# A new TensorE order table, new plan keys and another split of R tiles between VectorE and ScalarE in an attention plus two-FFN kernel

## The chip, the cores and the metric
The kernel runs on one core of a Trainium2 chip. The metric is device time in microseconds (us). Engines are named as in the profile: PE (TensorE matmul), PEld (its weight load), DVE (VectorE), ACT (ScalarE), POOL (GpSimd), SP (SyncE, which issues the DMAs).

## What is computed
Attention with a learned position bias, then two gated feed-forward networks, all in fp32 (2 batches, 8 heads, 576 positions, head width 64):

```python
x    = log1p(|i - j|) / log1p(max(i, 1))             # 576 x 576
bias = relu(x[..., None] @ w1 + b1) @ w2             # 32 hidden units -> 8 heads
e    = exp(s - max(s)), s = q @ k.T / 8 + bias
a    = (e / sum(e)) @ v                              # -> 1152 x 512
y    = (h * clip(h + 3, 0, 6) / 6) @ w_out,          h = a @ w_in
z    = rmsnorm(y) * g;  out = (silu(z @ w_gate) * (z @ w_val)) @ w_out2
```

## The kernel before
**Attention** is cut into 9 query tiles of 128 rows and, in each, 4 pairs of heads: 36 units, u = 0 to 35. A unit u is these blocks, which are also the names in the order table:
- S.u (`scores`, L440): four matmuls that multiply q by k for two heads; the two heads lie in the two row halves of the array. It writes two PSUM tiles `s`.
- softmax_d (L453, DVE, two per unit): adds the bias, writes e and the row extreme m. ACT then does exp (L464, two per unit).
- T.u.0, T.u.1, T.u.2 (`e_turn`, L101): 4, 4 and 1 transposes of e into PSUM (`tps`); e_copy (L484, DVE or ACT) evacuates each to `et`.
- PV.u (`pv`, L502): ten matmuls of v by `et`, accumulated in `pv`.

After the fourth unit of a tile come rps.t (transposes of the reciprocal sums) and on other engines rt, xf, xh (L540) and xl, which give the split input of the feed-forward networks. kT and qT are transposes of k and q; their evacuations are `kS` (L329) and `q` (L338).

**The bias** is made in 36 groups n of 16 positions. Each group needs four R tiles (`bias_R`: L357 on DVE, L352 on ACT, 128 rows by 304 to 576 columns), one block B.n of matmuls (L370), an evacuation `ev` in two parts (L393 on ACT, short parts L391 on DVE), a store to DRAM (L399) and, when eight groups are stored, loads back as `bias` (L425). Groups 16 to 23 come first; unit 0 waits for them.

**Order.** Every step has a key (PARAMS) and is emitted in order of key. Up to the key `man` that fixes the order on all engines. Behind it PE follows the table ORDER word for word, while a scheduler places the steps of the other engines, which work through their queues strictly in order. `START` and `MID` say by which engine (D is DVE, A is ACT) the four R tiles of a group are made; `ET` the same for e_copy by part and u mod 4, `KE` for the k evacuations, `XH` for xh. PSUM: two buffers for `s`, three for all transposes and the narrow B blocks, one for `pv`. SBUF: three `e`, three `et`, two `rawq`.

**The feed-forward networks** follow in a fixed order (L722, L767). Their weights are split into a high and a low part by ACT, DVE and POOL, a few of them already during attention.

Of the kernel before, what the change touches and what calls it, by code (L numbers as in the profile page):

```python
# [18 lines left out]
def shape_tables():  # L19
# [7 lines left out]


PARAMS = dict(
    g0=-5.972, gs=0.589, g8=-0.524, gt=-0.138, g14=1.055, gr=1.163, man=-0.96, zra=-0.643, zrd=-0.393, zrp=-1.107,  # L30
    zb=0.442, zev=0.711, zst=0.263, zevd=-77.57, zkt=-0.534, zkc=0.263, zqh=0.09, rd=-0.054, ra=-0.173, rp=0.346,
    b=0.242, ev=0.359, st=0.097, evd=82.888, k0=-5.351, k1=-3.46, k2=-2.983, k3=-0.198, k4=-0.333, k5=1.346,
    k6=2.548, k7=1.028, k8=2.644, lk=-2.593, cc=-5.654, kt=0.51, kc=0.179, lv0=0.532, lv1=1.209, q0=-3.292,
    q1=-0.365, q2=0.79, q3=4.828, lq1=-0.018, lq=-2.569, qa=0.311, qb=4.328, qh=0.06, bl=-5.532, s0=-0.452, s1=0.01,
    d0=0.245, d1=0.116, e0=0.934, e1=1.216, t0=0.919, t1=1.874, t2=1.529, c0=0.653, c1=0.389, c2=0.434, pv=2.825,
    ri=1.245, rb=1.468, rps=2.385, rt=2.634, xf=3.608, xh=4.242, xl=4.531, w=0.894, ws=0.496,
)

ORDER = """
kT.0,0,0 B.16 B.17 B.18 kT.0,1,0 B.19 kT.0,2,0 qT.0 B.21 B.22 B.23 B.20 S.0 B.13 B.12 B.11 B.10 B.9 kT.0,1,1  # L40
B.8 kT.0,0,1 qT.1 S.1 T.0.0 B.14 T.0.2 S.2 kT.1,0,0 T.1.0 T.0.1 kT.1,0,1 B.15 T.1.2 S.3 T.1.1 T.2.0 kT.1,1,0 B.24
kT.1,1,1 T.2.2 S.4 T.2.1 PV.0 PV.1 B.25 T.3.0 T.3.2 S.5 PV.2 qT.2 B.26 T.3.1 T.4.0 rps.0 T.4.2 S.6 B.27 B.28
PV.3 T.4.1 T.5.0 T.5.2 S.7 PV.4 T.5.1 T.6.0 T.6.2 S.8 PV.5 B.29 B.30 qT.3 T.7.0 T.7.2 T.6.1 S.9 PV.6 T.7.1
T.8.0 rps.1 T.8.2 S.10 T.8.1 B.32 B.31 PV.7 T.9.0 B.33 PV.8 T.9.1 T.9.2 S.11 T.10.0 T.10.2 S.12 T.11.0 qT.4
B.34 PV.9 T.10.1 T.11.2 S.13 PV.10 B.35 T.11.1 T.12.0 B.0 rps.2 T.12.2 T.13.0 S.14 PV.11 T.12.1 T.13.2 S.15 T.14.0
T.14.2 B.2 B.1 PV.12 T.14.1 T.13.1 S.16 PV.13 B.3 T.15.0 qT.5 T.15.2 S.17 B.4 PV.14 T.15.1 T.16.0 rps.3
T.16.2 S.18 B.5 PV.15 T.16.1 T.17.0 T.17.2 S.19 PV.16 T.17.1 T.18.0 B.7 T.18.2 B.6 S.20 PV.17 T.19.0 qT.6 
T.18.1 T.19.2 S.21 PV.18 T.19.1 T.20.0 rps.4 T.20.2 S.22 PV.19 T.20.1 T.21.0 T.21.2 S.23 PV.20 T.21.1 T.22.0 T.22.2
S.24 PV.21 T.22.1 T.23.0 qT.7 T.23.2 S.25 PV.22 T.23.1 T.24.0 rps.5 T.24.2 S.26 PV.23 T.24.1 T.25.0 T.25.2
S.27 PV.24 T.25.1 T.26.0 T.26.2 S.28 PV.25 T.26.1 T.27.0 qT.8 T.27.2 S.29 PV.26 T.27.1 T.28.0 rps.6 T.28.2  # L50
S.30 PV.27 T.28.1 T.29.0 T.29.2 S.31 PV.28 T.29.1 T.30.1 T.31.0 T.30.0 T.30.2 S.32 PV.29 T.31.2 S.33 PV.30
T.31.1 rps.7 T.32.0 T.32.2 S.34 PV.31 T.32.1 T.33.0 T.33.2 S.35 PV.32 T.33.1 T.34.0 T.34.2 PV.33 T.34.1 T.35.0 T.35.2
PV.34 T.35.1 rps.8 PV.35
"""

START = ["DDDD", "DDAA", "DDAD", "DDDA", "DDDD", "DDDA", "DDDA", "DDDD"]
MID = ["DDDD", "DDDA"]
ET = ["DADA", "DAAA", "DAAD"]
KE = ["D", "D"]
RB, RT, XH, XL = "PADP"  # L60
SLOTS = dict(wr=3, na=0, nb=8, ns=29, far=8)
BUFS = dict(rawk=3, rawq=2, qp=2, bp=5, ep=3, etp=3, sm=3, Rp=12, evp=4, xa=1, ps_s=2, ps_t=3, ps_v=1)

# [2 lines left out]
def kernel(ctx, tc, q, k, v, w1, b1, w2, w_in, w_out, w_gate, w_val, w_out2, rms_g, dtab, ntab, itab, out):  # L66
# [170 lines left out]
    if True:  # L237
# [333 lines left out]
        def at(key, name, needs, fn, *args):  # L571
            plan.append((key, len(plan), name, needs, fn, args))
# [10 lines left out]
        for i, n in enumerate(n for c in order for n in range(8 * c, min(8 * c + 8, NG))):  # L583
            g = group_key(i)
            z = "z" if i < 8 else ""
            R_eng[n] = "".join(sorted(START[i] if i < 8 else MID[i % len(MID)], key="PDA".index))
            for j, x in enumerate(sorted(range(4), key=lambda x: "PAD".index(R_eng[n][x]))):
# [14 lines left out]
        for i, (x, key) in enumerate(KK.items()):  # L602
# [329 lines left out]
```

## Time and profile before

| | us |
|---|---|
| median of 3 runs | 650.74 (650.61 to 651.8) |
| profiled execution | 649.78 |
| its span | 648.0 |
| first matmul of the feed-forward networks | 211.94 |

PE is busy for most of the span. A busy time says that an instruction was under way, not that the engine ran at its best rate; where a block of always the same matmuls takes longer than elsewhere, it waited inside. The start of unit u is found on PE's timeline as the u-th row group `s<-kS,q`: unit 5 starts at 53.25, unit 6 at 61.17, unit 22 at 149.76 us.

### The profile page before, as it was taken

To read this page: it belongs to the slowest core of one execution; us is meant where nothing else is said; L and a number is where in the kernel's file an instruction comes from. 1 tells how busy PE (TensorE), PEld (TensorE's weight loads), DVE (VectorE), ACT (ScalarE), POOL (GpSimd) and SP (SyncE) were. 2 spreads that over 40 slices of the span, in tenths; PEclk is the share of its full clock that TensorE was granted. 3 is DMA by queue.
4 is the path that set the end of the run, shared out by engine and by line. 5 is a ranking of instruction groups with operands and counts; after the bars stand their busy time and mean duration, and the time that the engine had idled before them with its cause. 6 is when DMAs were issued, how large, how long until landed. Compare 5 with 4: busy or idle time off the path is not lost.

```text
span 648.0 us, 10847 instructions
## 1 busy us (share of the span) xinstructions
PE 616.8 (95%) x4136; PEld 518.6 (80%) x4136; DVE 460.6 (71%) x852; ACT 335.6 (52%) x691; POOL 143.3 (22%) x114
## 2 busy tenths in 40 slices
PE   4688889998999999999999999999999999999997
PEld 2245556666777999999999999999899999999996
DVE  6975897757564899888843799969766761387812
ACT  4766757777665565555534555564444441253511
POOL 1000100113110243333310023423332330032400
PEclk9989999999999999999999999999999999999999
DMA  6998965537200244434320134443433340154301
GB/s 151 271 258 245 293 206 156 144 102 184 94 1 2 66 141 147 121 121 124 127 66 1 33 99 130 130 130 98 133 128 119 108 148 16 33 177 150 98 1 49
DMA packets 73952, 77.78 MB, mean 120 GB/s; under 512 B 31916, under 2 KB 58668, under 8 KB 73900
## 3 DMA queue, kind: packets, MB, share of 16 engines
q1 hardware_dynamic: 73636, 77.02, 40.2%
q8 instruction: 32, 0.52, 0.3%
q14 instruction: 20, 0.16, 0.1%
q10 hardware_dynamic: 264, 0.07, 0.0%
HBM read 63.83 MB, written 13.25 MB: 119 GB/s over the span
## 4 chain that ended last, share of the span: by engine, by line
PE 80%; ACT 5%; DVE 4%; DMA 4%; SPq 3%; issue 2%; POOL 0%; ACTq 0%; POOLq 0%; DVEq 0%
PE h L722 39%; PE ya L767 18%; PE yb L767 9%; PE s L440 5%; PE pv L502 3%; PE tps L101 3%; ACT e L464 3%; PE bps L370 2%; DVE e L453 2%; SPq L305 1%; DVE R L357 1%; ACT ev L393 1%; DMA rawq<-in_q_dram 1%; DMA raw<-in_moe_w_out_dram 1%; ACT et L484 1%
## 5 line engine op out<-in xcount | busy, mean ns | idle before, releaser
L166 POOL TENSOR_TENSOR wl<-wm,wh 128x512 fp32r<-128x512 f32 x85 | 125.5, 1477 | 298.8 <-ACT wh L137 184.2
L158 DVE SCALAR_TENSOR_TENSOR wm<-raw,wm 128x512 int32<-128x512 int32 x85 | 120.6, 1419 | 0.9
L731 ACT CAST gh<-r 128x384 fp32r<-128x384 f32 x84 | 43.2, 514 | 115.7 <-DVE r L754 68.8
L722 PE MATMUL h<-nh,wh 128*128 128x384 f32 x288 | 97.2, 338 | 0.0
L722 PE MATMUL h<-nh,wl 128*128 128x384 f32 x288 | 96.7, 336 | 0.0
L722 PE MATMUL h<-nl,wh 128*128 128x384 f32 x288 | 96.5, 335 | 0.0
L464 ACT ACTIVATE e<-e,m 128x576 f32<-128x576 f32 x72 | 55.4, 770 | 48.6 <-DVE m L453 48.6
L722 PE MATMUL h<-xh,wh 128*128 128x384 f32 x192 | 65.4, 340 | 0.0
L754 DVE TENSOR_TENSOR r<-r,h 128x384 f32<-128x384 f32 x36 | 19.9, 553 | 63.1 <-PE h L722 63.1
L722 PE MATMUL h<-xh,wl 128*128 128x384 f32 x192 | 64.7, 337 | 0.0
L722 PE MATMUL h<-xl,wh 128*128 128x384 f32 x192 | 64.5, 336 | 0.0
L453 DVE CUSTOM_DVE_ANT_0 e<-s,bias 128x576 f32<-128x576 f32 x72 | 51.7, 754 | 16.6 <-PE s L440 14.8
L154 DVE SCALAR_TENSOR_TENSOR wm<-raw,wm 128x512 int32<-128x512 int32 x85 | 60.9, 716 | 2.8
L734 DVE TENSOR_TENSOR gl<-r,gh 128x384 fp32r<-128x384 f32 x84 | 46.6, 555 | 16.8 <-ACT gh L731 16.8
L145 ACT ACTIVATE wm<-raw 128x512 f32<-128x512 f32 x85 | 57.2, 674 | 2.2 <-DMA raw<-in_moe_w_in_dram 1.3
L101 PE MATMUL tps<-ident,e 128*128 128x128 f32 x324 | 49.3, 284 | 7.1 <-ACT et L484 4.1
L722 PEld LDWEIGHTS h<-nh,wh 128*128 128x128 f32 x288 | 54.1, 188 | 2.3 <-DVE nl L831 0.9
L357 DVE TENSOR_SCALAR R<-T,NB 128x320 f32<-128x320 f32 (+17 forms) x124 | 49.9, 460 | 8.3 <-PE bps L370 8.2
L722 PEld LDWEIGHTS h<-nl,wh 128*128 128x128 f32 x288 | 54.1, 188 | 1.4
L722 PEld LDWEIGHTS h<-nh,wl 128*128 128x128 f32 x288 | 54.0, 188 | 0.0
L101 PEld LDWEIGHTS tps<-ident,e 128*128 128x128 f32 x324 | 35.6, 142 | 22.6 <-ACT et L484 7.5
L137 ACT CAST wh<-wm 128x512 fp32r<-128x512 f32 x85 | 52.3, 618 | 1.0 <-DVE wm L158 0.9
(95 smaller groups left out, 1051.3 us busy)
## 6 DMA issues: line engine op xcount, KB each, us to landing
raw<-in_moe_w_out_dram SPq DMA_DIRECT2D x33, 512.0 KB, 3.6
biasd<-ev SPq DMA_DIRECT2D x36, 295.5 KB, 4.2
raw<-in_moe_w_in_dram SPq DMA_DIRECT2D x18, 512.0 KB, 3.6
raw<-in_moe_w_gate_dram SPq DMA_DIRECT2D x18, 512.0 KB, 3.5
bias<-biasd SPq DMA_DIRECT2D x15, 576.0 KB, 4.5
raw<-in_moe_w_val_dram SPq DMA_DIRECT2D x16, 512.0 KB, 3.6
bias<-biasd SPq DMA_DIRECT2D x10, 288.0 KB, 3.9
rawk<-in_k_dram SPq DMA_DIRECT2D x18, 128.0 KB, 3.8
```

The source lines that it names most:

```text
L101: nc.tensor.transpose(out, in_, ident[:n, :n])
L137: nc.scalar.copy(out=hi, in_=m)
L145: nc.scalar.activation(out=m, in_=raw[:, :, 1].bitcast(F32), func=ACTF.Abs, scale=2.0 ** -112)
L154: nc.vector.scalar_tensor_tensor(out=m, in0=raw[:, :, 0], scalar=29, in1=m, op0=ALU.logical_shift_right, op1=ALU.bitwise_or,)
L158: nc.vector.scalar_tensor_tensor(out=m, in0=raw[:, :, 1], scalar=-0x80000000, in1=m, op0=ALU.bitwise_and, op1=ALU.bitwise_or,)
L166: nc.gpsimd.tensor_tensor(out=lo, in0=m, in1=hi, op=ALU.subtract)
L357: nc.vector.tensor_scalar(out=R, in0=src, scalar1=NB1[:, col], scalar2=None, op0=ALU.max)
L453: nc.vector.tensor_tensor_reduce(out=e_t[u][:, a, :].rearrange("p (z j) -> p z j", z=2), in0=s[:, :, :SH], in1=bt[u][:, a, :].rearrange("p ...
L464: nc.scalar.activation(out=e_t[u][:, a, :], in_=e_t[u][:, a, :], func=ACTF.Exp, scale=-1.0, bias=m_t[t][:, h:h + 1], accum_out=sum_t[t][:, ...
L722: nc.tensor.matmul(ps, lhsT=w[wz][:, c * 128:(c + 1) * 128], rhs=x[xz][:, c, :], start=(i == 0), stop=(i == 11),)
L734: nc.vector.tensor_tensor(out=gl, in0=g, in1=gh, op=ALU.subtract)
L767: nc.tensor.matmul(y_t[ph, n, t], lhsT=g[gz][:, t * 128:(t + 1) * 128], rhs=w[wz], start=(f == 0 and i == 0), stop=(f == F - 1 and i == 2),)
```

## The change
It replaces numbers only: the keys in PARAMS, the table ORDER, and the lists START, MID, ET, KE and XH. All steps remain; one source line less shifts every line number by one (L453 becomes L452). The instructions of the feed-forward networks and their order on PE stay.

```diff
 PARAMS = dict(
-    g0=-5.972, gs=0.589, g8=-0.524, gt=-0.138, g14=1.055, gr=1.163, ...
+    g0=-6.008, gs=0.583, g8=-0.495, gt=-0.138, g14=1.165, gr=1.195, ...
...
 ORDER = """
-T.8.0 rps.1 T.8.2 S.10 T.8.1 B.32 B.31 PV.7 T.9.0 B.33 PV.8 T.9.1 T.9.2 S.11 T.10.0 T.10.2 S.12 T.11.0 qT.4
+B.32 B.31 PV.7 T.9.0 T.9.2 S.11 T.10.2 PV.8 T.10.0 B.33 T.9.1 S.12 qT.4 T.10.1 T.11.2 S.13 PV.9 B.35 T.12.0 T.11.0
...
-START = ["DDDD", "DDAA", "DDAD", "DDDA", "DDDD", "DDDA", "DDDA", "DDDD"]
-MID = ["DDDD", "DDDA"]
-ET = ["DADA", "DAAA", "DAAD"]
-KE = ["D", "D"]
-RB, RT, XH, XL = "PADP"
+START = ["DAAA", "DDDD", "DDDD", "DDDD", "DDDD", "DDAA", "DDDD", "DDDD"]
+MID = ["DDAA", "DDDA"]
+ET = ["DADA", "DAAA", "ADAD"]
+KE = ["D", "A"]
+RB, RT, XH, XL = "PAAP"
```

PE at the start of unit 1, from the k transpose just ahead of block B.8 (448 columns) on. `s<-kS,q` is a score block, `tps<-ident,e` transposes of e, `bps<-R,W2b` a B block. Before:

```order
L101 MATMUL kps<-ident,rawk 128x128 x4
L370 MATMUL bps<-R,W2b 32x448 x4
L101 MATMUL kps<-ident,rawk 128x128 x4
L101 MATMUL qps<-ident,rawq 128x128 x4
L440 MATMUL s<-kS_136,q 128x288 x4
L101 MATMUL tps<-ident,e 128x128 x4
L370 MATMUL bps<-R,W2b 32x352 x4
L101 MATMUL tps<-ident,e 128x128
L440 MATMUL s<-kS_136,q 128x288 x4
```

The change:

```order
L100 MATMUL kps<-ident,rawk 128x128 x4
L369 MATMUL bps<-R,W2b 32x448 x4
L100 MATMUL qps<-ident,rawq 128x128 x4
L100 MATMUL kps<-ident,rawk 128x128 x8
L100 MATMUL tps<-ident,e 128x128
L439 MATMUL s<-kS_136,q 128x288 x4
L369 MATMUL bps<-R,W2b 32x352 x4
L100 MATMUL tps<-ident,e 128x128 x4
L439 MATMUL s<-kS_136,q 128x288 x4
```

The score block of unit 1 now stands behind two more k transposes and behind the part T.0.2, which reads both halves of e of unit 0; before, it stood ahead of every transpose of e.

DVE around the R tiles of 560 and 576 columns. `e,m<-s,bias` is softmax_d, `R<-T,NB` an R tile, `wm` a weight being split. Before:

```order
L484 COPY et<-tps 128x512
L357 TENSOR_SCALAR R<-T,NB_114 128x560 x4
L391 TENSOR_SCALAR ev<-bps,INV 128x79
L158 SCALAR_TENSOR_TENSOR wm<-raw,wm 128x512
L391 TENSOR_SCALAR ev<-bps,INV 128x63
L531 TENSOR_TENSOR xf<-pv,rt 128x512
L357 TENSOR_SCALAR R<-T,NB_114 128x576
L540 CAST xh_75<-xf 128x4x128
L357 TENSOR_SCALAR R<-T,NB_114 128x576
L391 TENSOR_SCALAR ev<-bps,INV 128x47
L357 TENSOR_SCALAR R<-T,NB_114 128x576 x5
L453 ISA e,m<-s,bias 128x576
```

The change:

```order
L356 TENSOR_SCALAR R<-T,NB_114 128x560 x2
L153 SCALAR_TENSOR_TENSOR wm<-raw,wm 128x512
L390 TENSOR_SCALAR ev<-bps,INV 128x79
L530 TENSOR_TENSOR xf<-pv,rt 128x512
L390 TENSOR_SCALAR ev<-bps,INV 128x63
L483 COPY et<-tps 128x128
L157 SCALAR_TENSOR_TENSOR wm<-raw,wm 128x512
L356 TENSOR_SCALAR R<-T,NB_114 128x576
L452 ISA e,m<-s,bias 128x576
L452 ISA m 128x1
L452 ISA e,m<-s,bias 128x576
L452 ISA m 128x1
```

Between two softmax pairs stood eleven R tiles on DVE, four of 560 and seven of 576 columns; now three stand ahead of the next pair, and of the remaining ones two and two follow behind it.

ACT at the same place. `e,sum<-e,m` is exp. Before:

```order
L464 ACTIVATE e,sum<-e,m 128x576 x2
L393 ACTIVATE ev<-bps,INV 128x512
L393 ACTIVATE ev<-bps,INV 128x528
L352 ACTIVATE R<-T,SC 128x576
L484 COPY et<-tps 128x512
L393 ACTIVATE ev<-bps,INV 128x544
L484 COPY et<-tps 128x512
L484 COPY et<-tps 128x128
L464 ACTIVATE e,sum<-e,m 128x576
```

The change:

```order
L144 ACTIVATE wm<-raw 128x512 x2
L463 ACTIVATE e,sum<-e,m 128x576
L351 ACTIVATE R<-T,SC 128x560 x2
L392 ACTIVATE ev<-bps,INV 128x512
L392 ACTIVATE ev<-bps,INV 128x528
L463 ACTIVATE e,sum<-e,m 128x576
L483 COPY et<-tps 128x512
L539 CAST xh_75<-xf 128x4x128
L351 ACTIVATE R<-T,SC 128x576
L483 COPY et<-tps 128x128
L463 ACTIVATE e,sum<-e,m 128x576 x2
L351 ACTIVATE R<-T,SC 128x576
```

ACT now makes five R tiles of 560 and 576 columns here instead of one; two of them and two `ev` parts stand between the two exp of one unit.

## Rows read from the trace of the kernel before

**Rows 1.** page, part 1: busy time, share of the span, instructions per engine
```profile
PE 616.8 (95%) x4136; PEld 518.6 (80%) x4136; DVE 460.6 (71%) x852; ACT 335.6 (52%) x691; POOL 143.3 (22%) x114
```

**Rows 2.** by stretch: busy us (instructions) of PE, PEld, DVE, ACT, POOL; PEclk, DMA
```profile
0.00:30.00 30.00, 18.09 (x148) 6.88 (x148) 22.70 (x68) 19.00 (x42) 2.34 (x13) 1.00 0.80 202
30.00:53.20 23.20, 19.06 (x152) 11.45 (x152) 17.26 (x46) 14.51 (x35) 0.66 (x1) 0.93 0.92 249
53.20:149.80 96.60, 88.23 (x881) 57.39 (x879) 72.51 (x182) 67.30 (x150) 11.90 (x11) 1.00 0.67 192
149.80:212.00 62.20, 60.24 (x729) 46.36 (x728) 35.90 (x95) 38.03 (x93) 6.93 (x7) 1.00 0.21 61
212.00:648.00 436.00, 431.21 (x2233) 396.51 (x2232) 312.18 (x465) 196.81 (x374) 121.53 (x82) 1.00 0.32 100
```

**Rows 3.** the same for instructions on R tiles alone: PE, PEld, DVE, ACT
```profile
0.00:30.00 30.00, 12.51 (x112) 2.97 (x112) 18.24 (x55) 5.65 (x10) 1.00 0.80 202
30.00:53.20 23.20, 3.96 (x32) 0.68 (x32) 5.58 (x15) 1.31 (x2) 0.93 0.92 249
53.20:149.80 96.60, 18.37 (x208) 5.32 (x208) 26.13 (x55) 5.84 (x8) 1.00 0.67 192
```

**Rows 4.** groups by shape, 0-212 us: busy us, mean ns | idle before
```profile
L329 DVE COPY kS<-kps 128x512 f32<-128x512 f32 x8 | 5.5, 685 | 1.3 <-PE kps L101 1.2
...
L526 ACT COPY rt<-rps 128x512 f32<-128x512 f32 x9 | 5.2, 581 | 0.4 <-PE rps L101 0.3
...
L357 DVE TENSOR_SCALAR R<-T,NB 128x432 f32<-128x432 f32 x7 | 2.7, 437 | 0.0
...
L352 ACT ACTIVATE R<-T,SC 128x432 f32<-128x432 f32 x1 | 0.7, 654 | 0.0
```

**Rows 5.** timeline of ACT, 22-31 us: start, us, what [idle before <-releaser]
```profile
22.81 0.91 ACT L393 ACTIVATE ev<-bps,INV 128x224 f32<-128x224 f32 x2 [1.76 <-DMA biasd<-ev]
...
25.88 1.70 ACT L393 ACTIVATE ev<-bps,INV 128x192 f32<-128x192 f32 x4 [0.66 <-DMA biasd<-ev]
...
30.78 0.78 ACT L464 ACTIVATE e<-e,m 128x576 f32<-128x576 f32 x1 [0.53 <-DVE m L453]
```

**Rows 6.** timeline of PE between two score blocks, 53 to 62 us
```profile
53.25 1.24 PE L440 MATMUL s<-kS,q 64*128 64x288 f32 x8
...
57.38 0.63 PE L101 MATMUL qps<-ident,rawq 128*128 128x128 f32 x4 [1.65 <-DMA rawq<-in_q_dram]
...
60.47 0.63 PE L101 MATMUL rps<-ident,rb 128*128 128x128 f32 x4 [0.58 <-issue]
...
61.17 1.24 PE L440 MATMUL s<-kS,q 64*128 64x288 f32 x8
```

**Rows 7.** timeline of DVE, 66 to 96 us
```profile
66.97 2.29 DVE L357 TENSOR_SCALAR R<-T,NB 128x512 f32<-128x512 f32 x3
...
87.47 1.77 DVE L357 TENSOR_SCALAR R<-T,NB 128x560 f32<-128x560 f32 x4
...
92.17 3.02 DVE L357 TENSOR_SCALAR R<-T,NB 128x576 f32<-128x576 f32 x5
95.11 0.75 DVE L453 CUSTOM_DVE_ANT_0 e<-s,bias 128x576 f32<-128x576 f32 x1
```

**Rows 8.** timeline of ACT, 70 to 96 us
```profile
70.03 0.78 ACT L464 ACTIVATE e<-e,m 128x576 f32<-128x576 f32 x1 [2.27 <-DVE m L453]
...
86.37 0.78 ACT L464 ACTIVATE e<-e,m 128x576 f32<-128x576 f32 x1 [2.20 <-DVE m L453]
...
95.90 0.78 ACT L464 ACTIVATE e<-e,m 128x576 f32<-128x576 f32 x1 [2.11 <-DVE m L453]
```

**Rows 9.** timeline of PE, two score blocks close together
```profile
93.04 1.24 PE L440 MATMUL s<-kS,q 64*128 64x288 f32 x8
...
95.92 1.91 PE L440 MATMUL s<-kS,q 64*128 64x288 f32 x8 [0.94 <-DVE m L453]
```

**Rows 10.** waits of PE, 150 to 212 us: total us, times, longest
```profile
PE tps L101 <- ACT et L484: 1.7, 6, 0.4
```

More of the change, by code (lines that the diff above doesn't have):

```diff
@@ L29 @@
 PARAMS = dict(
[L30 to L34, printed above, removed]
@@ L35 @@
-    d0=0.245, d1=0.116, e0=0.934, e1=1.216, t0=0.919, t1=1.874, t2=1.529, c0=0.653, c1=0.389, c2=0.434, pv=2.825,
-    ri=1.245, rb=1.468, rps=2.385, rt=2.634, xf=3.608, xh=4.242, xl=4.531, w=0.894, ws=0.496,
+    g0=-6.008, gs=0.583, g8=-0.495, gt=-0.138, g14=1.165, gr=1.195, man=-0.96, zra=-1.638, zrd=-0.49, zrp=-1.321,
+    zb=0.328, zev=0.771, zst=0.263, zevd=-77.57, zkt=-0.498, zkc=0.679, zqh=0.239, rd=0.065, ra=-0.056, rp=0.322,
+    b=0.372, ev=0.707, st=-0.004, evd=82.888, k0=-5.214, k1=-3.597, k2=-2.919, k3=0.568, k4=-0.347, k5=1.261,
@@ L37 @@
+    k6=2.588, k7=0.681, k8=2.692, lk=-2.593, cc=-5.816, kt=0.242, kc=-0.678, lv0=0.461, lv1=0.983, q0=-4.023,
+    q1=-0.56, q2=0.628, q3=5.804, lq1=-0.036, lq=-2.815, qa=0.417, qb=2.278, qh=0.965, bl=-5.35, s0=-0.043,
+    s1=0.381, d0=0.283, d1=0.659, e0=1.229, e1=1.572, t0=1.992, t1=1.874, t2=1.793, c0=0.767, c1=0.741, c2=-0.187,
+    pv=2.753, ri=0.666, rb=1.589, rps=2.464, rt=2.688, xf=4.008, xh=3.849, xl=6.122, w=-1.238, ws=0.454,
 )
 ORDER = """
-kT.0,0,0 B.16 B.17 B.18 kT.0,1,0 B.19 kT.0,2,0 qT.0 B.21 B.22 B.23 B.20 S.0 B.13 B.12 B.11 B.10 B.9 kT.0,1,1
@@ L41 @@
-B.8 kT.0,0,1 qT.1 S.1 T.0.0 B.14 T.0.2 S.2 kT.1,0,0 T.1.0 T.0.1 kT.1,0,1 B.15 T.1.2 S.3 T.1.1 T.2.0 kT.1,1,0 B.24
-kT.1,1,1 T.2.2 S.4 T.2.1 PV.0 PV.1 B.25 T.3.0 T.3.2 S.5 PV.2 qT.2 B.26 T.3.1 T.4.0 rps.0 T.4.2 S.6 B.27 B.28
-PV.3 T.4.1 T.5.0 T.5.2 S.7 PV.4 T.5.1 T.6.0 T.6.2 S.8 PV.5 B.29 B.30 qT.3 T.7.0 T.7.2 T.6.1 S.9 PV.6 T.7.1
-T.8.0 rps.1 T.8.2 S.10 T.8.1 B.32 B.31 PV.7 T.9.0 B.33 PV.8 T.9.1 T.9.2 S.11 T.10.0 T.10.2 S.12 T.11.0 qT.4
-B.34 PV.9 T.10.1 T.11.2 S.13 PV.10 B.35 T.11.1 T.12.0 B.0 rps.2 T.12.2 T.13.0 S.14 PV.11 T.12.1 T.13.2 S.15 T.14.0
@@ L46 @@
[L46 to L50, printed above, removed]
@@ L51 @@
-S.30 PV.27 T.28.1 T.29.0 T.29.2 S.31 PV.28 T.29.1 T.30.1 T.31.0 T.30.0 T.30.2 S.32 PV.29 T.31.2 S.33 PV.30
-T.31.1 rps.7 T.32.0 T.32.2 S.34 PV.31 T.32.1 T.33.0 T.33.2 S.35 PV.32 T.33.1 T.34.0 T.34.2 PV.33 T.34.1 T.35.0 T.35.2
-PV.34 T.35.1 rps.8 PV.35
-"""
-START = ["DDDD", "DDAA", "DDAD", "DDDA", "DDDD", "DDDA", "DDDA", "DDDD"]
-MID = ["DDDD", "DDDA"]
-ET = ["DADA", "DAAA", "DAAD"]
-KE = ["D", "D"]
-RB, RT, XH, XL = "PADP"
+kT.0,0,0 B.16 B.17 B.23 B.20 B.13 B.22 S.0 B.18 kT.0,1,0 B.12 B.9 kT.0,2,0 B.11 qT.0 B.19 B.10 kT.0,0,1 B.8 B.21 qT.1
@@ new lines @@
+kT.0,1,1 kT.1,0,1 T.0.2 S.1 B.14 T.0.0 S.2 kT.1,0,0 T.0.1 T.1.1 S.3 kT.1,1,0 S.4 T.1.2 T.2.2 kT.1,1,1 T.1.0 B.15 T.2.1
+T.2.0 PV.0 B.24 B.26 T.3.2 PV.1 S.5 PV.2 T.4.1 T.3.0 B.25 qT.2 rps.0 T.3.1 T.4.0 B.27 T.5.0 T.4.2 S.6 B.28 PV.3 S.7
+PV.4 T.5.2 T.5.1 T.6.2 S.8 T.7.0 T.6.1 PV.5 qT.3 T.6.0 S.9 PV.6 T.7.2 B.29 B.30 T.8.0 rps.1 T.8.2 T.7.1 S.10 T.8.1
+B.32 B.31 PV.7 T.9.0 T.9.2 S.11 T.10.2 PV.8 T.10.0 B.33 T.9.1 S.12 qT.4 T.10.1 T.11.2 S.13 PV.9 B.35 T.12.0 T.11.0
+B.34 PV.10 T.11.1 T.12.2 S.14 PV.11 B.0 rps.2 T.13.0 T.13.1 T.12.1 S.15 T.13.2 T.14.0 B.2 B.1 PV.12 T.14.2 T.14.1 S.16
@@ new lines @@
+PV.13 B.3 T.15.0 T.16.0 B.4 qT.5 S.17 T.15.2 T.15.1 rps.3 T.16.2 S.18 B.5 PV.15 PV.14 T.17.1 T.16.1 T.17.0 T.17.2 S.19
+T.18.0 B.7 PV.16 PV.17 T.19.0 T.18.2 B.6 S.20 qT.6 T.19.1 T.19.2 S.21 T.18.1 T.20.0 rps.4 S.22 T.20.1 T.20.2 PV.18
+PV.19 T.21.2 T.21.0 S.23 PV.20 T.21.1 T.22.1 T.22.0 S.24 PV.21 T.22.2 qT.7 T.23.0 S.25 T.23.2 T.24.2 T.24.0 T.23.1
+rps.5 S.26 PV.22 PV.23 T.24.1 S.27 T.25.0 T.26.0 T.25.1 T.25.2 PV.24 S.28 T.26.2 T.27.1 qT.8 T.27.2 S.29 PV.25 T.27.0
+rps.6 T.26.1 T.28.0 T.28.2 S.30 PV.26 PV.27 T.29.2 T.28.1 T.29.0 S.31 T.30.2 T.30.0 T.29.1 PV.28 T.31.0 S.32 PV.29
@@ L61 @@
+T.30.1 T.31.2 T.31.1 rps.7 PV.31 T.32.2 T.32.1 S.33 PV.30 T.32.0 S.34 T.33.0 T.33.2 T.33.1 S.35 PV.32 T.34.0 T.34.2
+T.34.1 PV.33 T.35.2 T.35.1 T.35.0 PV.34 PV.35 rps.8
+"""
+START = ["DAAA", "DDDD", "DDDD", "DDDD", "DDDD", "DDAA", "DDDD", "DDDD"]
[3 more added lines that the diff above has]
+RB, RT, XH, XL = "PAAP"
 SLOTS = dict(wr=3, na=0, nb=8, ns=29, far=8)
```

## Prediction, made before the changed kernel ran
> **What bounds the kernel now.** I read the share of busy time first: PE 95% of the span [rows 1]. Then the engines stretch by stretch [rows 2]: from 212 us on, in the feed-forward networks, PE is busy 431.2 of 436.0 us, at the granted clock 1.00 (2.4 GHz). Their instructions and their order on PE stay, so I carry these 436.0 us over. Everything the change can give or take lies in the 212 us ahead of them. There PE is idle 11.9, 4.1, 8.4 and 2.0 us in the four stretches (30.00 - 18.09, and so on). 26.4 us is thus about the most that a better order could win, apart from waits inside a block, which count as busy.
>
> Who makes PE wait differs by stretch. Up to 30 us it is the start: DVE is busy 22.7 us, 18.2 of them R tiles [rows 2, 3], and the bias must go through DRAM before the first softmax. From 53.2 to 149.8 us DVE is the busiest engine behind PE, 72.5 of 96.6 us against 67.3 for ACT; 26.1 us are R tiles [rows 2, 3]. From 149.8 us on there are no R tiles any more and PE is nearly full.
>
> **The change, part by part.**
>
> *R tiles from DVE to ACT.* MID gave ACT one R tile in two groups; now it gives three. For the 28 groups behind the first eight that is 28 tiles moved; START gives one back. At 432 columns a tile takes 437 ns on DVE and 654 ns on ACT [rows 4]. In the stretch 53.2 to 149.8 us 63 tiles are made, so some 16 groups, 16 tiles moved: DVE loses 16 x 26.13/55 = 7.6 us, ACT gains 16 x 5.84/8 = 11.7 us [rows 3]. xh moves too, about four times in this stretch: at the 0.58 us of the nearest row on ACT, a copy of 128x512 [rows 4], that is 2.3 us more on ACT. ACT comes to 67.3 + 11.7 + 2.3 = 81.3 of 96.6 us, DVE to some 63. The most loaded helper is then ACT, not DVE.
>
> What DVE's relief is worth: exp waits for the softmax on DVE 2.27, 2.20 and 2.11 us at three places [rows 8]. At the first, three R tiles of 512 columns (2.29 us) run until just ahead of the softmax, and at the third eleven of 560 and 576 columns, of which four and five are shown (1.77 + 3.02 us), end as it begins [rows 7]. The wait at 86.37 us lies elsewhere and I leave it. In the new order of DVE three tiles stand ahead of the softmax at the third place instead of eleven, and at the first the 512 tiles stand on both sides of one. Eight tiles at 3.02/5 = 0.60 us are 4.8 us less ahead of the softmax; of that PE can only see the wait, about 2 us, and its follow-up: the score block at 95.92 us that waited 0.94 us and took 1.91 instead of 1.24 us, because it stands right behind the one at 93.04 us [rows 9]. The new table has three parts of T, a PV and a B block between these two, where the old one had two parts of T. I take 3.0 us for both places; bounds 0 (the wait only changes its name) and 6 (2.27 + 2.11 + 0.94 + 0.67).
>
> What it costs on ACT: in the order of ACT two R tiles and two long `ev` now stand between the two exp of one unit, 4 x 5.84/8 = 2.9 us if an `ev` of that width costs what an R tile does [rows 3]. T.u.1 of that unit stands so much later; but in the new table it mostly comes two score blocks behind S.u, and a unit lasts 5.5 us there ((149.76 - 61.17)/16), so most is hidden. I charge 1.2 us; bounds 0 and 5.4 (2.9 there and 1.2 to 1.3 at two smaller places, all in the open).
>
> Here a rule speaks against the change. The Trainium skill, "ScalarE: Activation LUTs", section Rules for kernel authors, says to give relu and max to VectorE and not to ScalarE. The rows agree in direction, 437 against 654 ns. By the rule alone the change only adds engine time, and the third of the rivals below would be the forecast.
>
> *The start.* Ahead of its first exp ACT gets six R tiles more, two k evacuations more (KE) and one q less: 6 x 5.65/10 + 2 x 0.58 - 0.58 = 4.0 us [rows 3, 4]. It has 1.76 + 0.66 + 0.53 = 2.95 us idle there, waiting for stores and for the softmax [rows 5]; the rest, 1.0 us, shows, and a further k evacuation stands between the first two exp, 0.6 us. The score block of unit 1 now waits for T.0.2, which needs both. So +1.6 us at unit 1. The softmax itself isn't earlier: it waits for the bias, which needs the same eight groups and stores. Behind it, up to unit 5, PE idles 4.1 us [rows 2]; four k evacuations fewer on DVE (0.685 us each, rows 4) take some of that: -1.6. Together 0; bounds -3 and +3.
>
> *Units 5 and 6.* PE waits 1.65 us for q of tile 2 and 0.58 us at rps [rows 6]. In the new order two of the v loads are issued before, so that this q load comes earlier in SP's queue, and its transposes stand behind more blocks of T and B. I take both waits as gone: -2.2; bounds -2.2 and 0.
>
> *From 149.8 us.* PE waits for et 1.7 us at six places [rows 10]. The old table mostly has one part of T and one score block between the last transposes of a unit and its PV, the new one often a further PV or further transposes. I take 1.2 of these 1.7 us as gone. Against it four pairs of score blocks (units 25, 28, 33, 34) have only transposes, or one PV and one part of T, between them, where the two softmax of 0.75 us [rows 7] must fit; a close pair cost 0.94 + 0.67 us [rows 9]. At a seventh of that each, since DVE has no R tiles there, +0.9 us. Sum -0.3; bounds -2 and +2.
>
> Sum: -3.0 + 1.2 + 0 - 2.2 - 0.3 = -4.3 us. The profiled execution took 649.78 us, its span 648.0; changed, 645.5. The median of the runs is 650.74, 0.96 above the profiled one, so I forecast 646.4 us.
>
> **The rivals.**
>
> *ACT becomes the bound.* From the point at which what stands between two exp of a unit exceeds the PE work up to its T.u.1, each microsecond on ACT shows. For it: 84% load, a strict queue, the 2.9 us above. Against it: two unit periods of cover. Then 5.4 us are lost instead of 1.2, the start keeps its +1.6 and gains nothing behind it, the DVE gain shrinks to 1.8 and only the q wait is saved: 5.4 + 1.6 - 1.8 - 2.2 = +3.0, so 653.7 us.
>
> *The waits only move.* PE also waits for `et`, `ev` and its own PSUM buffers; a wait for DVE that ends may be followed by one of these at the same time. The old and the new table have the same blocks, and the unit period is set by three engines with about the same load (PE 88, ACT 81 of 96.6 us). Gains of 2.2 and losses of 1.6 are left: about 650.2, no change.
>
> *DVE was the whole bound up to 150 us.* If every microsecond taken off DVE there shows, 7.6 + 1.7 (four xh at 0.42) = 9.3 are won, and 2.2 at q, less 1.6 at the start: -9.9, so 640.8 us. For it: 8.4 us idle of PE, and score blocks that take 1.9 instead of 1.24 us. Against it: only some of the waits of PE there name DVE.
>
> **How the numbers follow.** The forecast 0.47, with its own range 643 to 649.4; ACT as bound 0.20; waits that move 0.14; all of DVE's relief 0.19. A difference under 0.2%, 1.3 us, cannot be told from none. Faster: 0.47 and 0.19, 0.66; same 0.14; slower 0.20. The range for 8 in 10 reaches from 640 (the fourth case) to 653.5 (nearly the second).
>
> **What would show it.** Right: the first row `h<-xh,wh` at 207 to 208 us instead of 211.94, and 436 us behind it unchanged; exp's waits for the softmax around 70 and 95 us under 1 us; no wait of PE for q near 57 us; ACT busy some 81 us between units 5 and 22. Wrong: PE waiting there for exp or `ev`, the first score block of unit 1 later than 34 us without a return by unit 5, or a stretch from 150 us on that is longer than 62 us.

## The result, and the profile after

The changed kernel takes 643.79 us (median of 4 runs, 641.25 to 644.54) against 651.27 us for the kernel before on the same chip: the ratio is 0.9874, 95% interval 0.9839 to 0.9909, so 7.5 us are won. I had forecast 646.4 us in a range of 640 to 653.5, and faster with a chance of 0.66.

The profiled executions show less, 5.2 us of span (648.0 to 642.8). The profiled run of before, 649.78 us, lies 1.5 us under that kernel's median of the comparison, and the one of after, 644.54 us, 0.75 us above its own; 5.2 + 1.5 + 0.75 is the 7.5 us again. The mean granted clock of TensorE was 0.997 and 0.996 in the two, so the 5.2 us are no matter of the clock.

Share of the span and instructions by engine, page of the changed kernel:

```profile
PE 617.0 (96%) x4136; PEld 520.9 (81%) x4136; DVE 442.9 (69%) x813; ACT 356.8 (56%) x730; POOL 143.5 (22%) x114
```

PE has the same 617 us of work as in [rows 1]; the helpers have traded 18 us on DVE for 21 us on ACT. The five stretches are cut at the same events as [rows 2] (30 us, the score blocks of units 5 and 22, the first `h`). A row gives the length, then busy us (instructions) of PE, PEld, DVE, ACT and POOL, the granted clock of TensorE (1.00 is 2.4 GHz, 0.50 is 1.2 GHz), the share of time in which the DMA engines were busy, and GB/s:

```profile
0.00:30.00 30.00, 18.44 (x136) 7.08 (x140) 17.05 (x51) 20.56 (x44) 2.34 (x13) 1.00 0.83 203
30.00:53.60 23.60, 18.75 (x166) 11.61 (x166) 16.69 (x45) 20.09 (x47) 0.61 (x1) 1.00 0.94 260
53.60:145.70 92.10, 87.76 (x864) 58.01 (x862) 62.20 (x162) 75.36 (x163) 8.07 (x9) 0.98 0.67 187
145.70:206.70 61.00, 60.77 (x750) 47.51 (x749) 34.93 (x92) 43.75 (x104) 10.56 (x10) 1.00 0.29 76
206.70:642.80 436.10, 431.29 (x2235) 396.71 (x2232) 312.01 (x465) 197.01 (x375) 121.89 (x82) 1.00 0.32 100
```

Read each row as length less PE's busy time. PE's idle time was 11.9, 4.1, 8.4, 2.0 us and is 11.6, 4.9, 4.3, 0.2 us: 5.4 us less in all, against 5.2 us of span. All of it lies between unit 5 and the feed-forward networks, 4.0 us ahead of unit 22 and 1.7 us behind it (up to unit 5 PE idles 0.4 us more); the feed-forward networks take 436.1 us as before. (The two tables don't have quite the same blocks between two events, so idle time is the measure, not length. Waits inside a block, and matmuls at a lower clock, count as busy.)

What PE waited for between units 5 and 22, before (us in total, times, longest):

```profile
PE tps L101 <- ACT et L484: 2.4, 3, 1.4
PE qps L101 <- DMA rawq<-in_q_dram: 1.6, 1, 1.6
PE tps L101 <- ACT ev L393: 1.4, 1, 1.4
PE s L440 <- DVE m L453: 0.9, 1, 0.9
PE bps L370 <- DVE m L453: 0.7, 2, 0.5
PE rps L101 <- issue: 0.6, 1, 0.6
```

and after:

```profile
PE rps L100 <- issue: 1.7, 1, 1.7
PE tps L100 <- DVE et L483: 1.4, 1, 1.4
PE s L439 <- DVE ev L390: 0.5, 1, 0.5
PE bps L369 <- DVE m L452: 0.3, 1, 0.3
PE tps L100 <- ACT q L337: 0.2, 1, 0.2
```

The waits for `et` on ACT, for q's load and for `ev` on ACT are gone. Two new ones stand together, 1.4 us at 79 us and 1.7 us at 81 us, and ACT's timeline (start, us, what, idle before) shows what is beside them:

```profile
77.76 0.66 ACT L144 ACTIVATE wm<-raw 128x512 f32<-128x512 f32 x1 [3.89 <-DMA raw<-in_moe_w_in_dram]
78.32 0.76 ACT L463 ACTIVATE e<-e,m 128x576 f32<-128x576 f32 x1
...
86.24 0.78 ACT L463 ACTIVATE e<-e,m 128x576 f32<-128x576 f32 x1 [0.25 <-DVE m L452]
...
87.38 1.42 ACT L351 ACTIVATE R<-T,SC 128x560 f32<-128x560 f32 x2 [0.27 <-PE bps L369]
...
89.85 0.77 ACT L463 ACTIVATE e<-e,m 128x576 f32<-128x576 f32 x1
```

The first conversion of a weight waits 3.89 us for its load, and the exp behind it in ACT's queue waits too, though its softmax was done at 75.2 us. DVE's next step on that weight waits 2.56 us for the conversion, and the evacuation of `et`, to which PE's wait at 79 us is put down, stands behind it:

```profile
74.45 0.76 DVE L452 CUSTOM_DVE_ANT_0 e<-s,bias 128x576 f32<-128x576 f32 x1 [0.47 <-PE s L439]
...
78.45 0.43 DVE L152 TENSOR_SCALAR wm<-wm 128x512 int32<-128x512 int32 x1 [2.56 <-ACT wm L144]
78.79 0.28 DVE L483 COPY et<-tps 128x128 f32<-128x128 f32 x1
```

Right behind these two waits of PE the granted clock falls:

```profile
82.00:85.00 3.00, 3.00 (x14) 2.34 (x14) 2.31 (x6) 2.65 (x6) 0.00 (x0) 0.52 0.83 300
```

At 86 us the two exp of one unit stand 3.6 us apart with the R tiles between them, as I had foreseen; no PE wait answers to that.

### The profile page after: what moved, and what is told of

Its sections match the earlier page's. It is cut to its first block, busy times and chain, and to the rows that moved or that the text cites. A ratio compares the mean times of both kernels' runs of the same rounds, so it can differ in the third digit from the quotient of the medians.

```text
span 642.8 us, 10866 instructions
## 1 busy us (share of the span) xinstructions
PE 617.0 (96%) x4136; PEld 520.9 (81%) x4136; DVE 442.9 (69%) x813; ACT 356.8 (56%) x730; POOL 143.5 (22%) x114
## 4 chain that ended last, share of the span: by engine, by line
PE 91%; DMA 3%; ACT 2%; DVE 2%; issue 1%; ACTq 0%; SPq 0%; DVEq 0%
PE h L721 39%; PE ya L766 18%; PE yb L766 9%; PE pv L501 6%; PE s L439 6%; PE tps L100 6%; PE bps L369 5%; DMA biasd<-ev 1%; DMA raw<-in_moe_w_in_dram 1%; ACT ev L392 1%; PE rps L100 1%; DMA b1c<-in_b_dram 1%; PE xnT L100 1%; DVE R L356 1%; DVE e L452 1%
## 5 line engine op out<-in xcount | busy, mean ns | idle before, releaser
L721 PE MATMUL h<-nl,wh 128*128 128x384 f32 x288 | 96.6, 335 | 0.0
L452 DVE CUSTOM_DVE_ANT_0 e<-s,bias 128x576 f32<-128x576 f32 x72 | 52.0, 755 | 30.2 <-PE s L439 21.7
L721 PEld LDWEIGHTS h<-nh,wh 128*128 128x128 f32 x288 | 54.1, 188 | 2.3 <-DVE nl L830 0.9
L721 PEld LDWEIGHTS h<-nl,wh 128*128 128x128 f32 x288 | 54.1, 188 | 1.4
L721 PEld LDWEIGHTS h<-nh,wl 128*128 128x128 f32 x288 | 54.1, 188 | 0.0
L741 ACT ACTIVATE r<-h,half_c 128x384 f32<-128x384 f32 x48 | 27.7, 577 | 47.1 <-PE h L721 46.9
L749 ACT ACTIVATE r<-h 128x384 f32<-128x384 f32 x36 | 17.7, 492 | 64.9 <-PE h L721 64.9
```

Of the source, the lines that this page charges most:

```text
L452: nc.vector.tensor_tensor_reduce(out=e_t[u][:, a, :].rearrange("p (z j) -> p z j", z=2), in0=s[:, :, :SH], in1=bt[u][:, a, :].rearrange("p ...
L721: nc.tensor.matmul(ps, lhsT=w[wz][:, c * 128:(c + 1) * 128], rhs=x[xz][:, c, :], start=(i == 0), stop=(i == 11),)
```

## The experiments

In what follows the lists are START, MID, ET, KE and the letter of xh; the keys are the numbers in PARAMS; the table is ORDER, the order of TensorE. Each ratio is to the kernel before on the same chip, beside which the version ran. That kernel's own medians were 651.27 to 652.39 us there, so versions are compared by their ratios. The theories' figures in us start from 651.27. Three theories stood against each other at first: A, R tiles taken off DVE pay; B, the table pays; C, lists and table only fit each other.

**Lists alone**, on the kernel before:

```diff
-START = ["DDDD", "DDAA", "DDAD", "DDDA", "DDDD", "DDDA", "DDDA", "DDDD"]
-MID = ["DDDD", "DDDA"]
+START = ["DAAA", "DDDD", "DDDD", "DDDD", "DDDD", "DDAA", "DDDD", "DDDD"]
+MID = ["DDAA", "DDDA"]
 # and ET, KE, XH of the new kernel
```

> The kernel before with the new lists START, MID, ET, KE and XH; table and keys stay old. Before 651.27 us, changed 643.79. Theory A (the R tiles that leave DVE make most of the gain): 645.5 to 648. Theory B (the new table makes it): 650 to 652. Theory C (lists and table fit only each other): above 652, since 27 more tiles on ACT then hit a table that was not laid out for them.

Measured 649.86 us (12 runs), ratio 0.9963 (0.9947 to 0.9979). From 651.27 us that is 648.9, between A's range and B's: the lists alone give 0.2 to 0.5% of the 1.26%. C falls, since they don't lose.

**Lists back**, on the new kernel (the same lines the other way round):

> The changed kernel with the old lists; table and keys stay new. Theory A: 648.5 to 651, the DVE waits of exp are back. Theory B: 644 to 646.5. Theory C: above 651.

646.46 us, 0.9929 (0.9901 to 0.9957): the upper end of B's range; some 0.5% belong to the lists in this table too. Table and keys alone, with the old lists, leave 2.0 us of idle time between units 5 and 22, where the kernel before has 8.4 [rows 2]:

```profile
57.70:145.90 88.20, 86.22 (x862) 56.82 (x860) 68.51 (x179) 63.32 (x141) 8.13 (x9) 1.00 0.68 193
```

**MID back**, on the new kernel: the 28 tiles return to DVE, nothing else.

```diff
-MID = ["DDAA", "DDDA"]
+MID = ["DDDD", "DDDA"]
```

> The changed kernel with only MID old, so that 28 R tiles go back from ACT to DVE. Theory A: 647 to 650, and exp waits for the softmax on DVE some 20 us in the stretch of units 5 to 22 instead of 7.2. Theory B: within 1.5 us of 643.8. Theory C: above 650.

644.13 us, 0.9883 (0.986 to 0.9906) against 0.9874: the 28 tiles are worth nothing that can be measured. Theory A falls, and with it my largest term. Its stretches from 30 us to the first `h` (columns as in [rows 2]):

```profile
30.00:58.20 28.20, 22.64 (x167) 13.68 (x165) 18.39 (x50) 18.99 (x45) 0.61 (x1) 0.82 0.97 252
58.20:146.40 88.20, 86.65 (x864) 57.25 (x862) 67.09 (x176) 65.29 (x145) 7.82 (x9) 1.00 0.66 189
146.40:208.30 61.90, 61.01 (x749) 47.49 (x748) 34.92 (x92) 44.38 (x105) 10.57 (x10) 1.00 0.28 75
```

In the profiled runs the nothing is a difference of two things. Between units 5 and 22, for the same 864 matmuls, this kernel takes 88.2 us and idles 1.6 (88.20 - 86.65), where the new one takes 92.1 and idles 4.3. There the moved tiles cost 3.9 us: 2.8 of idle time and 1.1 of PE's busy time, with a granted clock of 0.98 for the stretch. But this kernel comes to unit 5 at 58.2 instead of 53.6 us, with a granted clock of 0.82 instead of 1.00 on the way. How much it usually loses there isn't shown: the profiled run, 646.16 us, lies 2.0 us above the median of its six, with a mean clock of 0.991 where the others have 0.994 to 0.996.

**Table back**, on the new kernel (lists and keys stay new):

> The changed kernel with the old table ORDER; lists and keys stay new. Theory A: 644.5 to 647. Theory B: 649 to 652. Theory C: above 651.

648.96 us, 0.9954 (0.9935 to 0.9973), or 648.3 from 651.27, just under B's range: 0.8% of the 1.26% is the table's. Step by step from the kernel before, the lists give 0.37%, the keys 0.09% more (0.9963 to 0.9954, far inside the noise) and the table 0.80% more. Its stretches:

```profile
30.00:56.70 26.70, 22.71 (x162) 13.84 (x160) 15.72 (x42) 20.20 (x48) 0.65 (x1) 0.81 0.85 233
56.70:149.20 92.50, 86.74 (x880) 57.11 (x879) 63.51 (x163) 78.11 (x170) 11.90 (x11) 1.00 0.68 197
149.20:211.40 62.20, 60.24 (x729) 46.35 (x728) 34.40 (x91) 40.18 (x97) 6.94 (x7) 1.00 0.21 61
```

The last row is that of [rows 2] to the second digit in PE's time, though ACT has other work: the 2.0 us of idle time behind unit 22 come with the old table. With the new table it is 0.2 us, but 0.9 with MID back and 1.3 with the old lists, so the lists have a part in it. In the middle this kernel idles 5.8 us, 2.6 less than before, with the old table. The same table with the new lists but the old keys (lists alone, above) idles 8.2 us there and shows q's wait, and this kernel doesn't. Lists alone:

```profile
59.47 0.63 PE L101 MATMUL qps<-ident,rawq 128*128 128x128 f32 x4 [2.19 <-DMA rawq<-in_q_dram]
62.56 0.63 PE L101 MATMUL rps<-ident,rb 128*128 128x128 f32 x4 [0.58 <-issue]
```

Table back:

```profile
59.41 0.63 PE L101 MATMUL qps<-ident,rawq 128*128 128x128 f32 x4 [0.25 <-DVE m L453]
62.51 0.63 PE L101 MATMUL rps<-ident,rb 128*128 128x128 f32 x4 [0.58 <-issue]
```

The 0.58 us at `rps` stay with the old table. That the keys gain q's wait isn't shown: this q load is issued at 56.16 us in the one and at 56.21 in the other, and its transposes run at 59.47 and 59.41. What differs is that PE comes to unit 5 at 54.8 us with the old keys and at 56.7 with the new, too late to wait.

**New MID for the first groups alone.** If the moved tiles help at the start and cost behind it, they should be moved only where they help:

```diff
-... START[i] if i < 8 else MID[i % len(MID)] ...
+... START[i] if i < 8 else (["DDAA", "DDDA"] if i < 14 else ["DDDD", "DDDA"])[i % 2] ...
```

> The new kernel, with the new MID only for the six groups 8 to 13, whose R tiles stand around the first softmaxes, and the old MID (DDDD, DDDA) for groups 14 on. Theory D: taking R tiles off VectorE pays at the start, where it gives the first softmaxes earlier (31.7 against 32.5 us) and keeps the clock at 1.00, and costs in the middle, where ScalarE's queue is held up (3.9 us at the weight's load); the two cancelled in the run with the old MID throughout. Then this kernel beats both: unit 5 at 53.6 to 55 us, units 6 to 22 in 80 to 81.5 us instead of 83.5, time 0.983 to 0.985 of the kernel before. Theory F: what is won at either place is lost at the next wait, the weights' loads and the bias's loads setting the end; then 0.987 to 0.989, like the two others. Theory A (the 28 tiles off VectorE are what pays, behind the start): 0.990 or more.

642.67 us, 0.9858 (0.9836 to 0.9881), between D's and F's figures. The stretches are those of D:

```profile
30.00:54.70 24.70, 19.41 (x167) 11.65 (x166) 18.25 (x50) 18.61 (x45) 0.61 (x1) 1.00 0.93 250
54.70:143.30 88.60, 86.69 (x862) 57.18 (x860) 67.10 (x176) 65.15 (x145) 7.74 (x9) 1.00 0.68 195
143.30:204.40 61.10, 60.88 (x750) 47.56 (x749) 35.02 (x92) 43.84 (x104) 10.65 (x10) 1.00 0.29 76
```

1.9 us idle in the middle (new: 4.3), unit 5 at 54.7 us, the first `h` at 204.4 instead of 206.7. By its ratio it is some 1 us faster than the new kernel, but the two intervals overlap.

**A filler in the idle time at the start.** The kernel with MID back idles 3.5 us ahead of T.0.2; the score block behind takes 2.29 us:

```profile
31.81 1.42 PE L100 MATMUL kps<-ident,rawk 128*128 128x128 f32 x8
36.75 0.47 PE L100 MATMUL tps<-ident,e 128*128 128x128 f32 x1 [3.51 <-ACT e L463]
37.15 2.29 PE L439 MATMUL s<-kS,q 64*128 64x288 f32 x8
```

The new kernel at the same place:

```profile
31.31 1.38 PE L100 MATMUL kps<-ident,rawk 128*128 128x128 f32 x8
35.10 0.33 PE L100 MATMUL tps<-ident,e 128*128 128x128 f32 x1 [2.42 <-DVE R L356]
35.36 1.24 PE L439 MATMUL s<-kS,q 64*128 64x288 f32 x8
```

On the kernel with MID back:

```diff
             ps = ps_t.tile([128, 4, 128], F32, tag="t", name="tps")
+            if (u, part) == (0, 2):
+                for x in range(16):
+                    transpose(ps[:, 1 + x % 3, :], ident)
```

> The new kernel with the old MID throughout, and 16 transposes of the identity, whose result nobody reads, put ahead of block T.0.2, into the 3.5 us in which TensorE idled before it (33.2 to 36.8 us); behind that idle time the granted clock was 0.5 for some 6 us. Theory G: the start of that kernel is late because of the clock after the idle time, not because of the bias. Then S.1 takes 1.24 us and not 2.29, the clock stays at 1.00 to 52 us, unit 5 starts at 54 to 56 us instead of 58.2, and of these 2 to 4 us at least half is left at the end: 0.983 to 0.986 of the kernel before, against 0.988. Rival H: the loads of the bias and ScalarE's queue set the start; the clock may stay up, unit 5 stays at 57 us or later, and the time 0.987 to 0.990.

642.54 us, 0.9854 (0.983 to 0.9878), against 0.9883 without the filler: G's range, though the intervals overlap. Stretches behind the idle time, MID back:

```profile
36.00:40.00 4.00, 3.25 (x17) 1.57 (x17) 1.33 (x4) 0.96 (x3) 0.00 (x0) 0.50 0.97 289
40.00:44.00 4.00, 4.00 (x29) 2.48 (x22) 2.53 (x8) 3.17 (x8) 0.00 (x0) 0.76 1.16 343
```

and with the filler:

```profile
36.00:40.00 4.00, 4.00 (x33) 2.42 (x30) 3.46 (x9) 2.54 (x7) 0.00 (x0) 1.00 1.03 329
40.00:44.00 4.00, 2.71 (x19) 1.58 (x17) 3.05 (x10) 3.66 (x9) 0.00 (x0) 1.00 1.13 265
```

The third number from the right is the granted clock: 0.50 (1.2 GHz) behind 3.5 us of idle time, 1.00 (2.4 GHz) with the filler. Unit 5 starts at 53.1 instead of 58.2 us; of these 5 us 3.7 are left at the first `h`, and by the ratios 1.9 in the time (the profiled run without the filler lies 2.0 us above its median).

**The same in the kernel before**, whose own idle time at unit 1 was 1.18 us ahead of the score block and 1.30 us inside it:

```diff
+            if u == 1:
+                fill = ps_v.tile([128, 4, 128], F32, tag="v", name="fill")
             ...
                     for a in range(2):
+                        if u == 1 and z == 0:
+                            for x in range(10):
+                                transpose(fill[:, x % 4, :], ident)
```

> The kernel before, all its orders untouched, with twice ten transposes of the identity, whose result nobody reads, in the two stretches in which TensorE idled at unit 1 (1.2 us ahead of its score block and 1.3 us inside it). Over its runs the kernel before had a mean granted clock of 0.9925 and the new one 0.997. Theory K: about 2 of the new kernel's 7.5 us are clock, not order: the new start idles in other places and the granted clock dips less often. Then the filled kernel shows 0.996 to 1.000, no dip at 32 to 44 us, and 0.9965 to 0.998 of the time before. Rival L: the clock's dips stretch only work that waits for the bias and the helpers anyway; then the clock may rise, but the time stays within 0.2% of before (0.998 to 1.002).

650.58 us (12 runs), 0.999 (0.9978 to 1.0003): L's range. Before, behind the place of the filler:

```profile
34.00:36.00 2.00, 2.00 (x10) 0.92 (x12) 1.77 (x5) 1.23 (x3) 0.00 (x0) 0.50 0.98 232
```

With the filler, there and behind the next idle time of PE:

```profile
34.00:36.00 2.00, 2.00 (x18) 1.12 (x19) 1.92 (x5) 1.12 (x3) 0.00 (x0) 1.00 0.99 202
...
38.00:40.00 2.00, 0.63 (x4) 0.42 (x4) 1.31 (x5) 1.54 (x4) 0.00 (x0) 1.00 1.11 354
40.00:44.00 4.00, 3.75 (x20) 1.94 (x21) 2.89 (x6) 2.53 (x7) 0.00 (x0) 0.63 0.94 212
```

In the profile the dip only moves: it now follows the idle time at 38 us. Over the runs the mean clock rose from 0.9944, that of the 17 runs of the kernel before beside it, to 0.9966, nearly the new kernel's 0.997, and the time fell by 0.9 us. Over all 49 runs of the kernel before in these experiments 0.001 of mean clock goes with 0.37 us, and their mean is 0.9932; from there to 0.997 makes 1.4 us. So 1 to 1.5 of the 7.5 us go with the clock, as an estimate; the rest doesn't.

**The table in two parts.** New up to the score block of unit 22, old from there (blocks already done left out):

```diff
+ ORDER = ...   # in words: new, up to "S.22", then old without what stands in that part
```

> The new kernel whose order table goes over to the old order from the score block of unit 22 on (blocks that the new order has done by then left out of the old). What the table gives from there on: from unit 22 to the feed-forward networks the kernel before took 62.2 us and the new one 61.0. If that part belongs to the table (my term for it was 0.3 of the 4.3 us), this kernel takes 62.2 there and is 1.1 us slower than the new one: 0.989. If the difference came from where the helpers stand at unit 22, it takes 61 there and the time is that of the new kernel, 0.987.

647.11 us, 0.9925 (0.9905 to 0.9945): 0.5%, some 3 us, slower than the new kernel, and worse than either expectation. Unit 22 to the first `h` takes 62.6 us. What PE waits for from unit 22 on:

```profile
PE tps L100 <- ACT et L483: 1.9, 6, 0.5
PE pv L501 <- ACT et L483: 0.3, 1, 0.3
```

The six waits of [rows 10] are back in an otherwise new kernel, where the trace of the new kernel lists none. They are 1.9 us of the 3. Where the rest comes from isn't shown; the seam between the two orders, which neither table has, may cost it.

Old up to unit 6, new from there:

> The new kernel whose order table is the old one up to the score block of unit 6 and the new one from there. The old table throughout cost 5 us (0.9954 against 0.9874). If the new table's gain is made in the units behind the start (units 6 to 22, 83.5 us against 86.0 with the old table, and 1.1 us from 22 on), this kernel keeps 3 to 4 us of the 5: 0.988 to 0.990. If it is made in the start (other blocks between S.0 and S.1, the idle time before T.0.2, the clock behind it), unit 6 starts at 63 us or later and most of the 5 us is gone: 0.992 to 0.996.

645.63 us, 0.9916 (0.9887 to 0.9946), between the two figures and with the widest spread of all (643.6 to 649.6). Its last stretch idles 0.2 us like the new kernel's. Its mean clock is 0.9915 over the runs, the new kernel's 0.997. In runs of about the same clock no cost of the old head shows: the three at 0.995 and 0.996 take 643.6 to 645.3 us, the new kernel's two at 0.996 take 644.4 and 644.5, and the profiled execution, at 0.996, comes to the first `h` at 205.7 us, not later than the new kernel's 206.7. As far as these runs show, what the old head costs goes with the clock.

**KE and XH back**, on the new kernel:

```diff
-KE = ["D", "A"]
-RB, RT, XH, XL = "PAAP"
+KE = ["D", "D"]
+RB, RT, XH, XL = "PADP"
```

> The new kernel with k's evacuations all on VectorE and xh on VectorE, as before (KE and XH back; START, MID, ET, keys and table stay new). START, KE, ET and XH together made 0.46% (0.9929 against 0.9883, both with the old MID). If KE and xh carry that: 0.990 to 0.992. If START or ET carries it: within 0.2% of the new kernel, 0.9855 to 0.9890. My prediction put xh on ScalarE as a load of 2.3 us there and no gain of its own, and the k evacuations as 1.6 us won by unit 5 and lost at unit 1: by it 0.987 to 0.988.

646.14 us, 0.9912 (0.9893 to 0.9931): these two lists seem to carry most of what START, KE, ET and XH give together (0.9929 against 0.9883). The profile doesn't place it well: from unit 6 to unit 22 both kernels take 83.5 us; this one comes to unit 6 at 64.9 instead of 62.2 us, with a clock of 0.72 at 32 to 44 us.

**Early tiles and filler together**:

> Both changes that gave something by themselves: the new MID only for groups 8 to 13 (0.9858 alone), and the 16 idle transposes ahead of T.0.2 (0.9854, on the old MID throughout). If the one shortens the idle time of TensorE at the start and the other only fills it, they pay for the same thing, the clock there: 0.9845 to 0.986, with a granted clock of 0.998 to 1.000. If they add: 0.982 to 0.9845. If the filler delays work on the path here, where the idle time is 1.6 us and not 3.5: 0.9865 or more.

643.08 us, 0.9884 (0.9862 to 0.9906). They don't add. In the profile the filler starts only at 34.1 us, since its buffer isn't free earlier, and delays unit 1 from 34.8 to 36.1 us: the last of the three expectations. With the early tiles alone the clock was at 1.00 in the start already, so the filler had nothing to win there.

**The same, with one evacuation of k moved to ScalarE**:

```diff
-... k_copy, x, z, KE[i % 2])
+... k_copy, x, z, "A" if x == (1, 1, 0) else KE[i % 2])
```

> As the run with both, and the evacuation of k's second quarter of tile set 1 (block kT.1,1,0) on ScalarE instead of VectorE, where it stands behind two softmaxes and the score block of unit 4 waits 1.64 us for it (46.22 us). On ScalarE 0.3 us are free there ahead of the next exp. If that wait is time on the path: 1.0 to 1.3 us less than the run with both, 0.002 lower. If the next exp or the next wait takes it over: the same within 0.1%.

642.2 us, 0.9856 (0.9838 to 0.9873). The wait that was to go, with the early tiles alone:

```profile
46.22 1.24 PE L439 MATMUL s<-kS,q 64*128 64x288 f32 x8 [1.64 <-DVE kS L328]
```

and now:

```profile
45.94 1.24 PE L439 MATMUL s<-kS,q 64*128 64x288 f32 x8 [1.73 <-ACT kS L328]
```

It has only changed engines. The time fell by about what I expected, but not for that reason; the mean clock is 0.9985 here and 0.9962 in the run with both, and the intervals overlap. By the ratios three of these four versions (early tiles, filler, both with this) lie at 0.9854 to 0.9858 and the one with both at 0.9884, around the new kernel's 0.9874; none is apart from it by its interval.

## Why the prediction was right, point by point

The time was near for reasons that were half mine, and so partly by luck: the largest term has no worth that can be measured, and places that I had priced too low or left out made up for it. The forecast of the profiled execution was 645.5 us, measured 644.54: -4.3 against -5.2 us. The first `h` stands at 206.7 us, just ahead of the 207 to 208 that I had named.

- *R tiles from DVE to ACT, -3.0 + 1.2 = -1.8.* Wrong in its mechanism. The observation came true: exp waits 0.86 us at 70.8 us, not at all around 93, and over the middle 21.4 us fell to 7.2. Before (54 to 150 us, by shape; the last figures are exp's wait for the softmax):

```profile
L464 ACT ACTIVATE e<-e,m 128x576 f32<-128x576 f32 x34 | 26.2, 770 | 21.4 <-DVE m L453 21.4
```

after:

```profile
L463 ACT ACTIVATE e<-e,m 128x576 f32<-128x576 f32 x37 | 28.6, 773 | 7.3 <-DVE m L452 7.2
```

  With MID back the sum is 13.4 us and PE idles less, not more. Exp's waits and PE's idle time between units 5 and 22 don't go together over these kernels:

| | exp waits, us | PE idles, us |
|---|---|---|
| before | 21.4 | 8.4 |
| lists alone | 11.9 | 8.2 |
| table back | 11.8 | 5.8 |
| lists back | 12.4 | 2.0 |
| MID back | 13.4 | 1.6 |
| new | 7.2 | 4.3 |

  An exp that starts earlier gives PE nothing where PE doesn't wait for it. I had priced ACT's waits, with one PE row [rows 9] beside them. The step that failed is "of that PE can only see the wait, about 2 us, and its follow-up". What the tiles cost in the middle, 2.8 us of idle time and 1.1 of busy time, is also more than my 1.2. It goes along with the weight's load at 77.76 us, for which ACT waits 3.89 us in the new kernel and 1.13 with MID back; that the load is the cause wasn't tried by itself.
- The rule I weighed, of the Trainium skill ("ScalarE: Activation LUTs", section Rules for kernel authors), to keep relu and max off ScalarE, thus points the right way for the middle. At the start the six tiles of groups 8, 10 and 12 do no harm on ScalarE (0.9858 with them, 0.9883 without). The rival that goes with the rule is the first, ACT as the bound, not the third as I wrote.
- *The start, 0 (bounds -3 and +3).* Unit 1 came at 35.4 us instead of my 32.4, and unit 5 at 53.6, 0.3 later than before. The size was right in this execution, the reason not: the first softmax came 1.7 us later, at 31.7, after a wait of 3.4 us for the load of the bias, and the return up to unit 5 is in part that the clock stayed at 1.00, where [rows 2] have 0.93. I didn't see the clock as a term. (One block of k transposes more stands ahead of unit 1 in the new table, six against five, not two more.)
- *Units 5 and 6, -2.2.* The two waits are gone, as I had said. The q load is issued at 52.7 us, 0.9 us ahead of unit 5, where before it was 0.9 us behind it (54.1), and the new table sets more blocks ahead of its transposes. What of that the keys gave isn't shown; by themselves they are worth nothing that can be measured (0.9963 to 0.9954).
- *From 149.8 us, -0.3.* The term that was too small. PE idles 0.2 us there instead of 2.0. All of the 1.7 us of [rows 10] is gone, not 1.2 of it, and of the +0.9 us that I charged for close score blocks nothing shows: a score matmul takes 429 ns there in both kernels.
- *What I left out.* The table's worth between units 6 and 22: with the old lists, old table and old keys idle 8.4 us from unit 5 to unit 22 [rows 2], new ones 2.0. And a gain from KE and xh, which I had counted only as load on ACT and within the start: without them the ratio is 0.9912, some 2.5 us more.

Of the rivals, ACT as the bound came partly: its load is 75.4 of 92.1 us (I had expected 81.3 of 96.6) and its wait for the weight goes along with PE's at 79 us, but 643.79 us are far from the 653.7. That all of DVE's relief shows is refuted by the run with MID back. That nothing is gained in the end was true of the 28 tiles, not of the whole.

## What to carry to other kernels

A wait of a helper is worth only what a row of the bounding engine's own waits shows beside it; price those rows first. The order written out for the bounding engine decided more here (0.8%) than which engine does the helpers' work (0.4 to 0.55%). Where an edit seems worth nothing, split it by place: two terms of opposite sign may cancel.

## What the runs showed of the hardware

The granted clock of TensorE fell to 0.50 behind idle stretches in the start, and in the new kernel behind two waits of 1.44 and 1.66 us at 79 to 81 us. The times of one kernel's runs go with it: of the kernel before, 648.3 us at a mean of 0.999, 653.8 at 0.988. How long PE idled in one stretch doesn't decide it by itself in these traces: 2.42 us ahead of T.0.2 left 1.00 in the new kernel, 2.53 us at the same place with KE and XH back was followed by a score block of 2.29 us, and in the kernel before 0.50 followed on idle times of only 1.18 and 1.30 us at unit 1. Work that nobody reads, put into the idle stretch, kept the clock up in one kernel (0.9883 to 0.9854) and only moved the dip to the next idle stretch in another (0.999).
